# Weights in three pieces, a first state in a bank of its own, and a new order of the first block, in a scan and gated network on one core

## The chip, the cores and the metric

One core of a Trainium2 chip runs the whole program. The metric is device time in microseconds (us). A core has a matrix engine (TensorE, PE in the profile; its weight loads are the row PEld), a vector engine (VectorE, DVE), a scalar engine (ScalarE, ACT), GpSimd (POOL) and SyncE (SP), which here only issues transfers. All work from queues of their own and wait for each other by semaphores. Matrix products land in PSUM, 8 banks of 2 KB per partition; everything else works on SBUF. Sixteen DMA engines move data, fed by queues: q1 (issued by SP), q10 (issued by ScalarE) and q0 (issued by POOL[...]).

## What is computed

The first stage is a linear recurrence with a state, in chunks (Mamba-2), over 4 batches, 8 heads, 768 tokens, head size 32, state size 16. The second is a gated feed-forward network on the 3072 tokens of 256 values, with 1536 hidden units.

```python
for c in range(nc):
    cum = np.cumsum(la, axis=-1)                      # la: log of the decays a
    L = np.exp(cum[..., :, None] - cum[..., None, :]) * causal
    M = np.einsum('bhin,bhjn->bhij', Cc, Bc) * L
    y_intra = np.einsum('bhij,bhjd->bhid', M, xc)
    y_inter = np.einsum('bhin,bhnd->bhid', Cc, state) * np.exp(cum)[..., None]
    y[:, :, sl] = y_intra + y_inter
    Bx = np.einsum('bhjn,bhjd->bhjnd', Bc, xc) * decay_from_j[..., None, None]
    state = decay_full[..., None, None] * state + np.sum(Bx, axis=2)
...
gate = np.maximum(x @ w_gate, 0.0)
out = (gate * (x @ w_val)) @ w_out
```

## The kernel before

**Tiling.** The scan runs in pairs of 128-token chunks, 12 pairs of 256 tokens, three to a batch. The network runs in 6 blocks of 512 tokens, so block 0 needs pairs 0 and 1. The hidden units are 12 tiles f of 128. Decays enter as running products that scale B and C (C by the product, B by its reciprocal), so that the chunk's product of C and B needs only a causal mask.

**A pair of batch 0.** The pairs 0 to 2 take a layout of their own ("wide"). The steps, by name: `load` (C, B and x), `scale_wide` (C or B times the factors `wfac`, the result is the tile bs), `transp` and `tevac` (transposes by TensorE into tp and tpb, copied to BT and CT), `G_wide` (the 4 products g of C and B, a PSUM bank each), `gcopy` and `gmask` (a product is copied by ScalarE and then masked, or masked straight out of PSUM; result gw), `cast_x` (x as bf16), `adds` (the chunk's addition A to the state), `carry` and `pass_on` (the running state T, and its decayed copy Sw for the next chunk), `inter_wide` (C on the old state) and `D_wide` (gw on x), both into the PSUM tiles y and Aps, and `yevac_wide` (the result to yT, the network's input). A of chunk 0 lies in columns 256 to 320 of the y bank. Later pairs use `scale_bc`, `G`, `sums`, `states`, `inter`, `Dm`, `yevac`.

**A block of the network.** `gv` does one tile f for 512 tokens: two products with w_gate, two with w_val, then ScalarE's Relu and VectorE's product (h). `gvh` does the same for one half of the tokens, so that it can start when only one pair is ready; with later=True it returns the VectorE step, to be called later. `fout(b, ts)` multiplies 12 tiles of h by w_out for 128 tokens, and `foevac` copies and stores two of these at a time.

**Order.** It is written out by hand: `in_order` (line 15) keeps every engine's instructions in the order of the program text. So a waiting instruction holds all behind it on its engine. The tile pools add the waits for data and for buffers. Five PSUM banks are shared (`bank`, line 66: dummies, factors, the g products, gv, gate, val, o); one each goes to tp, y and Aps.

**Transfers.** SP issues the loads of inputs; two of them are held by a one-element VectorE memset on their buffer (lines 83 and 96), so they go out only when VectorE has come to that place in its order. POOL issues the weights: `weights(f0, f1)` is one transfer of w_gate and one of w_val, `weights_out` one of w_out. POOL also scales and casts for pair 1 on.

**Dummies.** `keep_warm(n)` runs n products of zeros on TensorE, so that it is not idle while the first pair is prepared.

The main order around the change is at lines 645 to 779; from line 780 a loop does blocks 1 to 5, with the pairs of the next block in between.

Of the kernel before, what the change touches and what calls it, by code (L numbers as in the profile page):

```python
# [29 lines left out]
def kernel(  # L30
# [13 lines left out]
    nc = tc.nc  # L44
# [21 lines left out]
    def bank(name="bank", shape=(128, 512), dtype=FP32):  # L66
        return mm.tile(list(shape), dtype, tag="shared", bufs=NSHARED, name=name)
# [25 lines left out]
    def load_x(p, *qs):  # L93
        xr = raw.tile([128, NH, 2, D], FP32, tag="xr", name="xr")
        if p == 1:
            nc.vector.memset(xr[0:1, 0, 0, 0:1], 0.0)
        n = NH // len(qs)
        for i, q in enumerate(qs):
            hs = slice(i * n, (i + 1) * n)
            q.dma_start(out=xr[:, hs].rearrange("p h r d -> p h (r d)"),  # L100
                        in_=x[0, hs, p * 256:(p + 1) * 256, :].rearrange(
                            "h (p r) d -> p h (r d)", r=2))
        st.setdefault(p, {})["xr"] = xr
# [71 lines left out]
    nc.vector.tensor_copy(  # L175
        heads, oneh.rearrange("p (t q) -> p q t", t=2).to_broadcast([R, 4, 2, N]))

    def keep_warm(n, tag="shared"):
        if tag == "tp":
            w = mm.tile([128, 128], FP32, tag="tp", name="w")  # L180
        else:
            w = bank("w", (128, 128))
        for _ in range(n):
            nc.tensor.matmul(out=w, lhsT=warm, rhs=warm, start=True, stop=True)  # L184

    wg = glob.tile([128, 2, DF], BF16)
    wv = glob.tile([128, 2, DF], BF16)
# [2 lines left out]
    def weights(f0, f1):  # L190
        fs = slice(f0 * 128, f1 * 128)
        for w, src in ((wg, moe_w_gate), (wv, moe_w_val)):
            nc.gpsimd.dma_start(
                out=w[:, :, fs], in_=src[:, fs].rearrange("(k p) f -> p k f", k=2))

    def weights_out(f0, f1):
        nc.gpsimd.dma_start(
            out=wo[:, f0:f1, :],
            in_=moe_w_out[f0 * 128:f1 * 128, :].rearrange("(o i) m -> i o m", i=128))
# [21 lines left out]
    def decays(step):  # L221
        if step == 0:
            nc.vector.tensor_scalar_mul(ends, onew, cp0[:, 127:128])
            return
        d = bank("dec", (128, NC))
        nc.tensor.matmul(out=d, lhsT=heads.rearrange("p q t n -> p (q t n)"), rhs=ends,
                         start=True, stop=True)
        nc.scalar.copy(out=dec, in_=d)
# [8 lines left out]

    def middle():
        nc.vector.reciprocal(rmid, cp[:, H - 1:H])
        nc.vector.tensor_scalar_mul(pick[:, 0], pairs[:, 0], rmid)  # L240

    scaleBC = glob.tile([128, NB, NC, 2, 8], FP32)

# [59 lines left out]
    def cast_x(p, ceng):  # L303
        s = st[p]
        cast = ceng.copy if ceng is nc.scalar else ceng.tensor_copy
        xb = att.tile([128, 2 * NH * D], BF16, tag="xb", name="xb")
        if p < NWIDE:
            cast(xb, s["xr"].rearrange("s h r d -> s (h r d)"))
            s["xb"] = xb.rearrange("s (h r d) -> s h r d", h=NH, r=2)
        else:  # L310
            cast(xb, s["xr"].rearrange("s i h d -> s (i h d)"))
            s["x"] = [xb[:, i * NH * D:(i + 1) * NH * D] for i in range(2)]
# [14 lines left out]
    def tevac(p, beng, ceng):  # L327
# [21 lines left out]
        if p < 2:  # L349
            (beng.copy if beng is nc.scalar else beng.tensor_copy)(BT, tp[0])  # L350

# [16 lines left out]
    def gmask(p, q, eng, psum=False):  # L371
        s = st[p]
        d = s["gw"][:, q]
        m = wmask.unsqueeze(2).to_broadcast([128, 2, 2, 128])
        eng.tensor_tensor(out=d, in0=s["gp"][q] if psum else d, in1=m, op=ALU.mult)  # L375

    def gcopy(p, q):
        s = st[p]
        nc.scalar.copy(out=s["gw"][:, q], in_=s["gp"][q])
# [7 lines left out]
    def adds(p):  # L387
        y_wide(p)
        s = st[p]
        s["A"] = [s["yw"][i][:, 256:320] for i in range(2)]  # L390
        halves = [i for i in range(2) if 2 * p + i < NC - 1]
        for r in range(2):
            for i in halves:
                half = slice(64 * i, 64 * i + 64)
                for q in range(4):
                    nc.tensor.matmul(
                        out=s["A"][i][32 * q:32 * q + 32],
                        lhsT=s["bs"][half, r, 32 * q:32 * q + 32],
                        rhs=s["xb"].rearrange("s (t q) r d -> s q r t d", t=2)[half, q, r],
                        start=r == 0, stop=True,  # L400
                        tile_position=(64 * i, 32 * q), skip_group_check=True)
        for i in halves:
            s["begun"][i] = True

    S = {}
    T_ = {}
# [32 lines left out]
                        tile_position=(32 * q, 32 * q), skip_group_check=True)  # L439
            s["begun"][i] = True  # L440

    def D_wide(p):
        s = st[p]
        for t in range(2):
            for r in range(2):
                for i in range(2):
                    half = slice(64 * i, 64 * i + 64)
                    y = s["yw"][i][:, 0:256].rearrange("s (t m) -> s t m", t=2)
                    for q in range(4):
                        nc.tensor.matmul(  # L450
                            out=y[32 * q:32 * q + 32, t],
                            lhsT=s["xb"][half, 4 * t + q, r], rhs=s["gw"][half, q, r, t],
                            start=not s["begun"][i] and t == 0 and r == 0, stop=True,
                            tile_position=(64 * i, 32 * q), skip_group_check=True)

    def yevac_wide(p, *engs):
        s = st[p]
        for i, eng in enumerate(engs):
            dst = yT[:, :, p * 256 + i * 128:p * 256 + (i + 1) * 128]
            (eng.copy if eng is nc.scalar else eng.tensor_copy)(  # L460
                out=dst, in_=s["yw"][i][:, 0:256].rearrange("s (t m) -> s t m", t=2))
# [161 lines left out]
    def foevac(b, ts):  # L623
        last = b == NBLK - 1
        if ts % 2 == 0 and not last:
            return
        ob = ffn.tile([128, 2, DM], FP32, tag="ob", name="ob", bufs=3)
        r0 = b * 512 + ts * 128
        if last:
            i = ts % 2  # L630
            (nc.vector.tensor_copy if i else nc.scalar.copy)(out=ob[:, i], in_=fst["o"][:, i])
            (nc.sync if i else nc.scalar).dma_start(out=out[r0:r0 + 128, :], in_=ob[:, i])
            return
        nc.scalar.copy(out=ob, in_=fst["o"])  # L634
        nc.sync.dma_start(
            out=out[r0 - 128:r0 + 128, :].rearrange("(i p) m -> p i m", p=128), in_=ob)


    def turn(p, apart=False):
        transp(p, 1, apart)  # L640
        transp(p, 0, apart)

    V, A_, P_ = nc.vector, nc.scalar, nc.gpsimd

    keep_warm(20)
    d = factors()
    decays(0)
    decays(1)
    keep_warm(3)
    nc.vector.tensor_copy(wfac[:, 1], d)  # L650
    nc.gpsimd.tensor_copy(gate[:, 0:1], wfac[0:1, 1, 0, 0, 0:1])
    weights(0, 4)
    scale_wide(0, 1, V)
    nc.vector.reciprocal(wfac[:, 0, :, :, 0], wfac[:, 1, :, :, 0])
    scale_wide(0, 0, V)
    transp(0, 1, False)
    keep_warm(3)
    transp(0, 0, True)
    tevac(0, A_, V)
    nc.vector.reciprocal(wfac[:, 0, :, :, 1], wfac[:, 1, :, :, 1])  # L660
    scan(0, H)
    scale_wide(1, 1, P_)
    weights(4, 8)
    scale_wide(1, 0, P_)
    keep_warm(4)
    G_wide(0)
    keep_warm(16)
    gcopy(0, 0)
    gmask(0, 2, V, True)
    load_x(1, nc.sync)  # L670
    gcopy(0, 1)
    cast_x(0, A_)
    adds(0)
    keep_warm(3)
    gmask(0, 3, V, True)
    gmask(0, 0, V)
    gmask(0, 1, V)
    pass_on(0, 0)
    carry(0, 0)
    middle()  # L680
    inter_wide(0)
    D_wide(0)
    turn(1, True)
    yevac_wide(0, A_, V)
    carry(0, 1)
    weights(8, NF)
    cast_x(1, P_)
    weights_out(0, NF)
    tevac(1, V, A_)
    pass_on(0, 1)  # L690
    def halves(b, u, *fs):
        for f in fs:
            gvh(b, f, u)

    load(2)
    load(3)
    f0 = gvh(0, 0, 0, True)
    G_wide(1)
    decay()
    gcopy(1, 0)  # L700
    gmask(1, 2, V, True)
    f0()
    gcopy(1, 1)
    late = [gvh(0, 1, 0, True)]
    gmask(1, 3, V, True)
    late += [gvh(0, 2, 0, True)]
    adds(1)
    gmask(1, 0, V)
    gmask(1, 1, V)
    carry(1, 0)  # L710
    late += [gvh(0, 3, 0, True), gvh(0, 4, 0, True)]
    pass_on(1, 0)
    late += [gvh(0, 5, 0, True)]
    decay_factors()
    inter_wide(1)
    D_wide(1)
    for fin in late:
        fin()
    nc.vector.reciprocal(wfac[:, 0, :, :, 2], wfac[:, 1, :, :, 2])
    yevac_wide(1, A_, A_)  # L720
    halves(0, 0, 6, 7)
    carry(1, 1)
    pass_on(1, 1)
    load(4)
    load(5)
    scale_wide(2, 1, P_)
# [5 lines left out]
    smask = const.tile([128, 2, 128], BF16)  # L732
    for t in range(2):
        nc.gpsimd.tensor_scalar_mul(smask[:, t], bd, tmask[:, t:t + 1])
    halves(0, 1, 0, 1, 2, 3, 4, 5, 6, 7)
    gv(0, 8)
    gv(0, 9)
    turn(2)
    tevac(2, A_, A_)
    gv(0, 10)  # L740
    gv(0, 11)
    cast_x(2, P_)
    fout(0, 0)
    foevac(0, 0)
# [135 lines left out]
```

## Time and profile before

| What | Value |
|---|---|
| median of 9 runs (range) | 129.48 us (128.66 to 130.27) |
| the profiled execution: time / span | 129.25 us / 127.5 us |
| granted clock of TensorE | 0.997 of full |
| busy share of the span: PE / DVE / ACT / POOL | 95% / 69% / 64% / 31% |
| chain that ended last: PE / DMA / DVE / issue | 80% / 9% / 3% / 2% |
| bytes moved by q1 / q0 | 8.91 / 2.36 MB |
| first products of block 0 (gv) start | 11.19 us |
| first w_out product of block 0 (o) starts | 26.13 us |
| first products of block 1 (gv) start | 34.10 us |

The profile is one execution, in us from the span's start. The page cuts the span into 40 slices of 3.19 us; a digit is the busy share in tenths. A line of the timeline gives start, length, engine (ACTq, SPq and POOLq are issues), line of the program, operation, result and inputs with their shapes, how many instructions are merged (x16), and in brackets how long the engine was idle before and what ended that. A line of the chain gives start, length and what was worked on or waited for. A line of a DMA queue gives packets, MB, and the time of the packets as a share of 16 engines over the stretch asked for.

### The profile page before, as it was taken

Reading aid. Unit: us, or ns where it says so; the run is one execution under the profiler, and the core shown is the slowest. Engines: PE = TensorE matmul, PEld = TensorE weight load, DVE = VectorE, ACT = ScalarE, POOL = GpSimd, SP = SyncE. Lnnn points to the kernel's source line nnn. Section 1 sums busy time; section 2 is a strip of 40 time slices with the busy share of each in tenths; the row PEclk is TensorE's granted clock in tenths of the full one; section 3 lists DMA queues with packets and bytes.
Section 4 is the critical chain, followed back from the end, with each engine's and each line's share of the span. In section 5 each row is a group of like instructions: output and inputs, shape, how many; then the busy total and the mean of one; then the engine's idle time right before and its main releaser. Section 6 shows DMA issues by size and latency. Waiting matters only on the chain.

```text
span 127.5 us, 3631 instructions
## 1 busy us (share of the span) xinstructions
PE 120.9 (95%) x1381; PEld 84.6 (66%) x1387; DVE 88.5 (69%) x201; ACT 81.8 (64%) x186; POOL 40.1 (31%) x84
## 2 busy tenths in 40 slices
PE   6999899899999999999999999999999999999980
PEld 6765577368787468884477874577864677844770
DVE  4896957555799766798674989655989656688420
ACT  0567578654788843887845787935887746877310
POOL 6549402559175008620502802322600033000000
PEclk9999999999999999999999999999999999999998
DMA  3999999998899997197932289912200002200031
GB/s 65 213 152 178 176 212 202 137 126 97 100 114 214 110 124 97 58 162 95 110 50 87 75 108 106 109 27 82 82 5 0 0 0 87 82 0 0 5 115 50
DMA packets 72209, 12.15 MB, mean 95 GB/s; under 512 B 65936, under 2 KB 72192, under 8 KB 72192
## 3 DMA queue, kind: packets, MB, share of 16 engines
q1 hardware_dynamic: 66096, 8.91, 45.5%
q0 software_dynamic: 3184, 2.36, 13.0%
q10 hardware_dynamic: 2912, 0.66, 2.4%
q8 instruction: 11, 0.18, 0.6%
q14 instruction: 6, 0.05, 0.1%
HBM read 11.13 MB, written 3.15 MB: 112 GB/s over the span
## 4 chain that ended last, share of the span: by engine, by line
PE 80%; DMA 9%; DVE 3%; issue 2%; ACT 1%; POOL 1%; SPq 0%; DVEq 0%; POOLq 0%
PE o L618 25%; PE gv L600 16%; PE val L585 14%; PE gate L582 12%; DMA bcr<-in_B_dram 9%; PE w L184 3%; PE y L557 2%; PE tp L325 2%; PE g L469 2%; DVE gs L375 1%; PE y L546 1%; POOL bs L281 1%; PE g L362 1%; PE A_ps L516 1%; DVE h L589 1%
## 5 line engine op out<-in xcount | busy, mean ns | idle before, releaser
L589 DVE TENSOR_TENSOR h<-r,val 128x512 bf16<-128x512 bf16 x42 | 28.0, 684 | 9.6 <-ACT r L588 8.1
L618 PE MATMUL o<-wo,h 128*128 128x256 bf16 x288 | 34.3, 273 | 0.1
L618 PEld LDWEIGHTS <-h 128*128 128x128 bf16 x288 | 27.2, 98 | 5.3 <-issue 1.5
L588 ACT ACTIVATE r<-gate 128x512 bf16<-128x512 f32 x42 | 24.6, 601 | 5.6 <-PE gate L582 3.7
L606 DVE TENSOR_TENSOR h<-r,gv 128x256 bf16<-128x256 bf16 x60 | 23.6, 416 | 4.3 <-ACT r L603 3.7
L585 PE MATMUL val<-yT,wv 128*128 128x512 bf16 x84 | 25.0, 379 | 0.3
L603 ACT ACTIVATE r<-gv 128x256 bf16<-128x256 f32 x60 | 22.6, 384 | 3.3 <-PE gv L600 1.4
L582 PE MATMUL gate<-yT,wg 128*128 128x512 bf16 x78 | 23.7, 379 | 0.0
L600 PE MATMUL gv<-yT,wv 128*128 128x256 bf16 x120 | 22.9, 273 | 0.6 <-DMA wv<-in_moe_w_val_dram 0.6
L600 PE MATMUL gv<-yT,wg 128*128 128x256 bf16 x120 | 23.0, 273 | 0.2
L494 DVE TENSOR_TENSOR gs<-g,maskUT 128x512 bf16<-128x512 f32 x18 | 11.6, 686 | 11.8 <-issue 9.6
L477 POOL TENSOR_SCALAR_AFFINE_SELECT gs<-gs 128x512 bf16<-128x512 bf16 (+1 forms) x18 | 8.9, 520 | 33.0 <-ACT gs L488 33.0
L295 POOL TENSOR_TENSOR bs<-bcr,scaleBC 128x256 bf16<-128x256 f32 x18 | 11.0, 630 | 20.2 <-DMA bcr<-in_C_dram 11.5
L585 PEld LDWEIGHTS <-wv 128*128 128x128 bf16 x84 | 8.2, 98 | 9.9
L600 PEld LDWEIGHTS <-wv 128*128 128x128 bf16 x120 | 11.6, 98 | 2.3 <-DMA wv<-in_moe_w_val_dram 0.8
L600 PEld LDWEIGHTS <-wg 128*128 128x128 bf16 x120 | 11.0, 98 | 2.2 <-issue 0.2
L582 PEld LDWEIGHTS <-wg 128*128 128x128 bf16 x84 | 7.8, 98 | 6.5
L488 ACT CAST gs<-g 128x512 bf16<-128x512 f32 x9 | 5.3, 589 | 6.7 <-PE g L469 6.7
L634 ACT COPY ob<-o 128x512 f32<-128x512 f32 x10 | 5.8, 583 | 5.1 <-PE o L618 5.1
L570 ACT CAST yT<-y 128x512 bf16<-128x512 f32 x9 | 5.3, 585 | 5.2 <-PE y L557 2.5
L184 PE MATMUL w<-warm 128*128 128x128 bf16 x49 | 6.4, 311 | 1.1 <-DVE tmask L155 1.1
L281 POOL TENSOR_TENSOR bs<-bcr,wfac 128x128 bf16<-128x128 f32 x8 | 3.1, 407 | 10.3 <-DVE h L606 6.3
(100 smaller groups left out, 118.7 us busy)
## 6 DMA issues: line engine op xcount, KB each, us to landing
out_dram<-ob SPq DMA_DIRECT2D x10, 256.0 KB, 2.2
xr<-in_x_dram SPq DMA_DIRECT2D x19, 128.0 KB, 3.6
bcr<-in_C_dram SPq DMA_DIRECT2D x19, 64.0 KB, 3.3
bcr<-in_B_dram SPq DMA_DIRECT2D x19, 64.0 KB, 3.5
wg<-in_moe_w_gate_dram POOLq DMA_DIRECT2D x3, 256.0 KB, 5.5
wv<-in_moe_w_val_dram POOLq DMA_DIRECT2D x3, 256.0 KB, 6.0
wo<-in_moe_w_out_dram POOLq DMA_DIRECT2D x1, 768.0 KB, 11.6
xr<-in_x_dram SPq DMA_DIRECT2D x2, 256.0 KB, 8.1
```

What stands on the lines that cost most here:

```text
L184: nc.tensor.matmul(out=w, lhsT=warm, rhs=warm, start=True, stop=True)
L295: eng.tensor_tensor(out=bs.rearrange("s k (q t n) -> s k t q n", q=4, t=2)[:, :, t], in0=src[:, :, t], in1=f[:, :, 4 * t:4 * t + 4].to_bro ...
L477: nc.gpsimd.affine_select(out=dst, in_=dst, pattern=[[0, n], [1, 128]], compare_op=ALU.is_ge, fill=0.0, base=0, channel_multiplier=-1)
L494: nc.vector.tensor_tensor(out=d[:, q], in0=g[q], in1=m, op=ALU.mult)
L582: nc.tensor.matmul(out=g, lhsT=wg[:, k, fs], rhs=yT[:, k, tk], start=(k == 0), stop=(k == 1))
L585: nc.tensor.matmul(out=v, lhsT=wv[:, k, fs], rhs=yT[:, k, tk], start=(k == 0), stop=(k == 1))
L588: nc.scalar.activation(r, g, AF.Relu)
L589: nc.vector.tensor_tensor(out=fst[b][:, f], in0=r, in1=v, op=ALU.mult)
L600: nc.tensor.matmul(out=gv_[:, j], lhsT=w[:, k, fs], rhs=yT[:, k, tk], start=(k == 0), stop=(k == 1), skip_group_check=True)
L603: nc.scalar.activation(r, gv_[:, 0], AF.Relu)
L606: nc.vector.tensor_tensor(out=fst[b][:, f, u * 256:(u + 1) * 256], in0=r, in1=gv_[:, 1], op=ALU.mult)
L618: nc.tensor.matmul(out=o[:, ts % 2], lhsT=fst[b][:, f, ts * 128:(ts + 1) * 128], rhs=wo[:, f], start=(f == 0), stop=(f == NF - 1), skip_gr ...
```

## The change

It has eight parts, all before block 1.

1. The weights come as tiles 0-1, 2-5 and 6-11, not as three pieces of four tiles. The first two pieces are issued one after the other, the third after `load(2)` and `load(3)` in the text. w_out is issued later, behind a mask that POOL does for pair 1.
2. x of pair 1 is loaded earlier in the order, and so are the loads of pairs 2 and 3 (behind `yevac_wide(0)`).
3. Dummies: other numbers, and two groups that read a masked product (gw) instead of zeros, so that they start only when it is there.
4. A of chunk 0 gets a bank of its own, A0. `D_wide` can do some of the q apart.
5. `decays(1)` and the cast of x of pair 0 move to between the two copies of products on ScalarE; `middle` does its second step on POOL.
6. In pair 1 `adds` and the carry come earlier, one mask goes to POOL, and the first-half tiles 1 to 5 stand in another order.
7. Tiles 6 and 7 of block 0 are done for 512 tokens at a time, like 8 to 11.
8. The transposes of pair 2 come one tile f earlier, with its copies spread between the tiles that follow; the copy of the third and fourth o of block 0 is split in two.

```diff
-    def keep_warm(n, tag="shared"):
...
+    def keep_warm(n, rhs=warm):
+        w = bank("w", (128, 128))
         for _ in range(n):
-            nc.tensor.matmul(out=w, lhsT=warm, rhs=warm, start=True, stop=True)
+            nc.tensor.matmul(out=w, lhsT=warm, rhs=rhs, start=True, stop=True)
...
-        nc.vector.tensor_scalar_mul(pick[:, 0], pairs[:, 0], rmid)
+        nc.gpsimd.tensor_scalar_mul(pick[:, 0], pairs[:, 0], rmid)
...
+    def copy_B(p, eng):
+        s = st[p]
+        s["BT"] = BT = att.tile([128, 2, 128], BF16, tag="BT", name="BT")
+        (eng.copy if eng is nc.scalar else eng.tensor_copy)(BT, s["tp"][0])
+
+    def copy_C(p, t):
...
+        nc.scalar.mul(
+            s["CT"].rearrange("s t i m -> s t (i m)")[:, t].rearrange(
+                "s (m r) -> s m r", r=2),
+            s["tp"][1].rearrange("s r m -> s m r"), tmask[:, t:t + 1])
...
+        if p == 0:
+            s["A"][0] = bank("A0", (128, 2 * D))
...
-            s["begun"][i] = True
+            s["begun"][i] = p > 0 or i > 0
...
-    def D_wide(p):
+    def D_wide(p, qs=(0, 1, 2, 3)):
...
-                    for q in range(4):
+                    for q in qs:
...
         if ts % 2 == 0 and not last:
+            if ts and not b:
+                fst["ob"] = ob = ffn.tile([128, 2, DM], FP32, tag="ob", name="ob", bufs=3)
+                nc.scalar.copy(out=ob[:, 0], in_=fst["o"][:, 0])
             return
...
+        if b == 0 and ts == 3:
+            nc.scalar.copy(out=ob[:, 1], in_=fst["o"][:, 1])
+        else:
+            nc.scalar.copy(out=ob, in_=fst["o"])
...
-    keep_warm(20)
+    keep_warm(22)
     d = factors()
     decays(0)
-    decays(1)
-    keep_warm(3)
+    keep_warm(8)
...
-    weights(0, 4)
+    weights(0, 2)
+    weights(2, 6)
...
-    keep_warm(3)
+    keep_warm(4)
...
-    nc.vector.reciprocal(wfac[:, 0, :, :, 1], wfac[:, 1, :, :, 1])
+    nc.vector.reciprocal(wfac[:, 0, :, :, 1:3], wfac[:, 1, :, :, 1:3])
     scan(0, H)
     scale_wide(1, 1, P_)
-    weights(4, 8)
     scale_wide(1, 0, P_)
-    keep_warm(4)
+    load_x(1, nc.sync)
+    keep_warm(6)
     G_wide(0)
-    keep_warm(16)
+    keep_warm(7)
     gcopy(0, 0)
     gmask(0, 2, V, True)
-    load_x(1, nc.sync)
+    keep_warm(5, st[0]["gw"][:, 0, 0, 0])
+    cast_x(0, A_)
+    decays(1)
+    adds(0)
     gcopy(0, 1)
-    cast_x(0, A_)
-    adds(0)
-    keep_warm(3)
     gmask(0, 3, V, True)
+    keep_warm(4, st[0]["gw"][:, 3, 0, 0])
...
-    D_wide(0)
+    D_wide(0, (2, 3, 0))
+    D_wide(0, (1,))
     turn(1, True)
+    keep_warm(2)
     yevac_wide(0, A_, V)
+    load(2)
+    load(3)
     carry(0, 1)
-    weights(8, NF)
+    weights(6, NF)
     cast_x(1, P_)
-    weights_out(0, NF)
...
-    load(2)
-    load(3)
     f0 = gvh(0, 0, 0, True)
     G_wide(1)
     decay()
+    adds(1)
...
-    late = [gvh(0, 1, 0, True)]
     gmask(1, 3, V, True)
-    late += [gvh(0, 2, 0, True)]
-    adds(1)
+    carry(1, 0)
+    pass_on(1, 0)
+    gmask(1, 1, P_)
+    weights_out(0, NF)
     gmask(1, 0, V)
-    gmask(1, 1, V)
-    carry(1, 0)
-    late += [gvh(0, 3, 0, True), gvh(0, 4, 0, True)]
-    pass_on(1, 0)
-    late += [gvh(0, 5, 0, True)]
-    decay_factors()
+    late = [gvh(0, f, 0, True) for f in (1, 2, 3)]
     inter_wide(1)
     D_wide(1)
-    for fin in late:
+    late[0]()
+    late[1]()
+    yevac_wide(1, A_, V)
+    late += [gvh(0, f, 0, True) for f in (4, 5)]
+    for fin in late[2:]:
         fin()
-    nc.vector.reciprocal(wfac[:, 0, :, :, 2], wfac[:, 1, :, :, 2])
-    yevac_wide(1, A_, A_)
-    halves(0, 0, 6, 7)
-    carry(1, 1)
-    pass_on(1, 1)
+    decay_factors()
...
-    halves(0, 1, 0, 1, 2, 3, 4, 5, 6, 7)
+    halves(0, 1, 0, 1, 2, 3, 4, 5)
+    gv(0, 6)
+    carry(1, 1)
+    gv(0, 7)
+    pass_on(1, 1)
     gv(0, 8)
+    turn(2)
+    copy_B(2, A_)
     gv(0, 9)
-    turn(2)
-    tevac(2, A_, A_)
+    copy_C(2, 0)
     gv(0, 10)
     gv(0, 11)
+    copy_C(2, 1)
```

More of the change, by code (lines that the diff above doesn't have):

```diff
@@ L176 @@
         heads, oneh.rearrange("p (t q) -> p q t", t=2).to_broadcast([R, 4, 2, N]))
-    def keep_warm(n, tag="shared"):
[L179 to L182, printed above, removed]
+    def keep_warm(n, rhs=warm):
+        w = bank("w", (128, 128))
         for _ in range(n):
-            nc.tensor.matmul(out=w, lhsT=warm, rhs=warm, start=True, stop=True)
+            nc.tensor.matmul(out=w, lhsT=warm, rhs=rhs, start=True, stop=True)
     wg = glob.tile([128, 2, DF], BF16)
@@ L350, in tevac @@
             (beng.copy if beng is nc.scalar else beng.tensor_copy)(BT, tp[0])
+    def copy_B(p, eng):
[3 more added lines that the diff above has]
+    def copy_C(p, t):
+        s = st[p]
+        if t == 0:
+            s["CT"] = att.tile([128, 2, 2, 128], BF16, tag="CT", name="CT")
+        nc.scalar.mul(
+            s["CT"].rearrange("s t i m -> s t (i m)")[:, t].rearrange(
+                "s (m r) -> s m r", r=2),
+            s["tp"][1].rearrange("s r m -> s m r"), tmask[:, t:t + 1])
     def G_wide(p):
@@ L625, in foevac @@
         if ts % 2 == 0 and not last:
+            if ts and not b:
+                fst["ob"] = ob = ffn.tile([128, 2, DM], FP32, tag="ob", name="ob", bufs=3)
+                nc.scalar.copy(out=ob[:, 0], in_=fst["o"][:, 0])
             return
-        ob = ffn.tile([128, 2, DM], FP32, tag="ob", name="ob", bufs=3)
+        ob = fst.pop("ob", None) or ffn.tile([128, 2, DM], FP32, tag="ob", name="ob", bufs=3)
         r0 = b * 512 + ts * 128
@@ L633, in foevac @@
             return
-        nc.scalar.copy(out=ob, in_=fst["o"])
+        if b == 0 and ts == 3:
+            nc.scalar.copy(out=ob[:, 1], in_=fst["o"][:, 1])
+        else:
+            nc.scalar.copy(out=ob, in_=fst["o"])
         nc.sync.dma_start(
```

## The prediction

> **What bounds the kernel now.** I read the chain of waits first, then TensorE's weight loads and ScalarE in order of time, and last the DMA queues by stretch. The chain from 0 to 42 us:
>
> ```profile
> 10.20 0.79 POOL bs L281 x2
> 11.04 0.30 PE tpb L325 x2
> 11.37 0.29 DVE BT L350
> ...
> 12.13 11.18 DMA bcr<-in_B_dram
> ...
> 23.81 0.42 POOL bs L281
> 24.28 0.30 PE tp L325 x2
> ...
> 32.11 1.32 PE o L618 x12
> 33.46 0.59 ACT ob L634
> 34.10 1.96 PE gv L600 x16
> ```
>
> From 34.10 on the chain is TensorE nearly alone, and the change touches nothing there. So block 1's first gv, at 34.10, decides: each us by which it comes earlier shortens the span by one. Before it, one transfer (B of pair 2, issued 12.13, landed 23.31) releases the transposes. TensorE's stalls after its first gv at 11.16 stand in the weight loads:
>
> ```profile
> 15.49 0.11 PEld L600 LDWEIGHTS <-wv 128*128 128x128 bf16 x2 [0.84 <-DMA wv<-in_moe_w_val_dram]
> ...
> 24.27 0.11 PEld L325 LDWEIGHTS <-bs 128*128 128x128 bf16 x2 [0.71 <-POOL bs L281]
> ...
> 27.57 0.10 PEld L618 LDWEIGHTS <-h 128*128 128x128 bf16 x1 [0.36 <-DVE h L589]
> ```
>
> Up to that first gv TensorE mostly waits for a chain through ScalarE; the last two copies of the mask product stand ahead of the cast of x:
>
> ```profile
> 7.07 1.07 ACT L379 CAST gs<-g 128x512 bf16<-128x512 f32 x2 [0.75 <-PE g L362]
> 8.02 0.63 ACT L308 CAST xb<-xr 128x512 bf16<-128x512 f32 x1
> 9.19 0.31 ACT L424 ACTIVATE Sw<-y,dec 128x64 bf16<-128x64 f32 x1 [0.54 <-PE y L396]
> 9.40 0.20 ACT L413 COPY T<-y 128x64 f32<-128x64 f32 x1
> 10.56 0.37 ACT L460 CAST yT<-y 128x256 bf16<-128x256 f32 x1 [0.95 <-PE Aps L450]
> ```
>
> DMA engines, 12 to 15 us (weights alone, though C and B of pair 2 are issued) and 15 to 17.5 us (both queues):
>
> ```profile
> q0 software_dynamic: 534, 0.52, 112.7%
> ```
>
> ```profile
> q0 software_dynamic: 422, 0.41, 99.1%
> q1 hardware_dynamic: 778, 0.10, 35.3%
> ```
>
> The engines are full until 24.7 us, where W_out lands (issued 13.10, 11.6 us). q0 carries weights, q1 all inputs.
>
> [...]pair 2's C, issued 11.71, moves nothing before 15. So a queue of weights holds loads back for a while, and which comes first matters. [...]the separate bank for A0 buys little.
>
> **Part by part.** a) Prologue. 22 dummies for 20: 2 x 0.105 (2.05/20), and they end just where the scan releases the factors (LDW 3.33): +0.19. Eight dummies stand where decays(1) and three were, under VectorE's scaling: 0. Four and six for three and four, ahead of G: six end 0.1 after BT is there, so G comes at 6.65 for 6.37: +0.28, not a sum with the first but holding it. The copy gcopy(0,0) then ends at 7.9. New order on ScalarE: cast of x (0.63) to 8.43, then the copy of decays(1). That waits for dec's two fp32 matmuls, which stand behind five dummies reading the first copied block (7.94 to 8.45) plus a mode change (0.2) and 0.59: 9.19. Behind this waiting copy stand gcopy(0,1), pass_on, carry. ScalarE: dec 9.22 to 9.39, gcopy(0,1) to 9.87, Sw to 10.16 (before: 9.50). VectorE's mask of q=1 ends 10.5 (before 9.59), and D takes q=2,3,0 first, so it stays hidden. inter 10.22, D 10.55, yT on ScalarE 10.56+0.66=11.22, on VectorE to 11.70. First gv 11.82: **+0.66**. Bounds: 0 (dec's matmuls slip in earlier, dummies shorter) and +1.0[...]. I take +0.66, the worked chain.
>
> b) TensorE's order from first gv (T0=11.82) to block 1. Tiles: 0.435 per half (17.39 to 20.01: six), 0.865 per full one (22.17, 23.03). Six halves less eight and six full less four: same columns, 0. Walk: gv 0; G(1) at 12.43, behind CT, as before; decay 12.81 to 13.6; adds +0.35 (xb: POOL ends weights(6,12) 12.6, cast 13.2); gv 1 to 3 to 15.3; inter waits for pass_on(1,0) (carry 15.0, Sw 15.4), 15.5; D 15.9 to 16.15, its POOL mask (1.15, from 14.2) done 15.35; gv 4, 5 to 17.0. r(1 to 3) are queued on ScalarE ahead of yevac, so it runs 16.45 to 16.82 and VectorE's half to 16.93: just in time. Six second halves to 19.66, full 6, 7, 8 to 22.25, transposes 0.45, full 9, 10, 11 to 25.3: W_out product of block 0 starts at **25.3** (before 25.91/26.13, T0 11.16).
>
> What goes: the 0.84 at wv (tiles 2-5 are issued by 7.75, not 10.18; 1024 packets of tiles 0-5 are 1.9+3.2 us of full engines from 6.3, plus 1.1 for x of pair 1: landed by 13.5, needed 14.65). Small first pieces also end the wv wait of gv 0 (landing 11.38): 0.13, lost in T0. Tiles 6-11 need the total of weights that tiles 8-11 needed before (landed 18.6): I take 19.0, needed 19.7 and 20.1. pick on POOL: about 0.5 (0.49 on VectorE), bounds 0.15 and 0.8, under decay's start at 12.8.
>
> c) Pair 2. C, B, x issued at 11.8, 12.3, 12.9, as late as before (11.71). Gain: all weights ahead of them are through sooner (w 2-5 close behind 0-1, before q0 fell to 58.9% share between 9.5 and 12), so q1 starts at about 14 rather than 15, and W_out, issued at 15.3 for 13.1, starts only behind tiles 6-11 at 18. At 311 packets per us (778/2.5) beside weights, 4 us carry 1240 of the 2048 of C and B; the other 800 at 233 per us (before: about 1118 in 4.8 us beside W_out): 21.4, landed **22.2**, bs 23.0. PE wants it at 22.5: stall 0.6. If q1 starts at 13.4, as x of pair 1 did (1.5 us after issue), 1430 are through, landed 21.4, stall 0. I take 0.2. The DMA for the change at the upper end is in the rivals. W_out: before 7.0 us from last weight packet to landing; 18.0+7.0=25.0, needed 25.3 to 25.5: hidden, bounds 24.3 and 25.8.
>
> d) turn(2) between tiles 8 and 9, its copies between 9, 10 and 11: ScalarE has 0.6 of each 0.865, plus 0.37+0.84+0.35 over six periods: 5.2 of 5.6. The last h no longer comes late: -0.36. ob in halves: the bank of o is free 0.2 earlier, first gv of block 1 waits for it at 33.46 to 34.05: -0.2. Remaining from W_out product to block 1: 34.10-26.13-0.56=7.41. pair 3's loads, POOL's scale (30.04 before) and sums are needed some 1.2 earlier; their loads are in at 28.7: hidden with 0.3 to spare.
>
> Sum: 25.3+0.2 (B) +7.41=32.9, against 34.10: **-1.2**. On the profiled execution 129.25 (span 127.5 and 1.75 around it): 128.05; that execution lies 0.23 below the median of 129.48, so in the median of runs 128.05 to 128.3. Forecast **128.2**.
>
> **Rivals.** (1) The prologue costs nothing (chain a at its lower bound): gain 1.8, 127.4. For: dec's matmuls are small; against: three instructions stand behind its copy. (2) Transfer hidden or late all the same: B lands 22.3 to 23.1, or W_out at 26: stall 0.5 to 1.2, 128.6 to 129.4. For: bytes are the same and the engines are full from 6 to 24.7; against: order is better. (3) Slower: q1 does not start before 15[...]: 825 by 18.0, the other 1223 take 5.2 us, B lands 24.0, transposes at 25.0; now three full tiles stand behind them, not two, so the product starts at 27.8, block 1 at 35.2: +1.1, **130.35**. It decides from a landing of 23.0, where block 1 is back at 34.10. For: before, B landed at 23.31 after the same issue time. Against: W_out was in its way from 17.7.
>
> **Numbers.** Forecast 0.55, (1) 0.10, (2) 0.19, (3) 0.16. Below 0.5% (0.65 us) a measurement of this kernel cannot tell it from no change. Forecast and (1) are faster, of (2) 0.05; same 0.14; (3) is slower, 0.16. Own range of the forecast 127.7 to 128.6; for 8 in 10, 127.3 to 129.7.
>
> **What would show it.** First gv at 11.8; no DMA wait at wv; B of pair 2 landed by 22.2; weight loads of the transposes of pair 2 with less than 0.3 idle; product of block 0 at 25.5 with no wait for h; block 1 at 32.9. Wrong, if B lands after 23, if W_out ends the wait at 25.3, or if first gv comes past 12.5.

## The result, and the profile after

The changed kernel is slower: 131.6 us median of 17 runs (129.71 to 132.59), against 129.48 of 54; the ratio is 1.0114, with a 95% interval of 1.0084 to 1.0145. (The ratio leaves out executions in a slower state, the medians don't.) The profiled execution took 131.27 us, its span is 129.5. Block 1's first gv starts at 36.00, before at 34.10: all of the loss (1.9 of 2.0 us of span) is in front of block 1.

The chain of waits after, from 10 to 44 us (start, length, what was worked on or waited for):

```profile
11.86 3.14 issue
...
15.03 0.61 POOL xb L305
...
15.68 0.21 PE y L409 x4
...
15.94 2.67 PE gv L613 x12
...
28.58 1.32 PE o L631 x12
...
36.00 1.99 PE gv L613 x16
```

Pair 2's B and POOL's scale of it are gone from the chain. In their place stands the cast of pair 1's x, after 3.14 us of nothing, and then 12 products of gv, three half tiles, that take 2.67 us: 0.89 per half tile, twice the 0.435 of before. The timeline says what each waited for:

```profile
15.03 0.60 POOL L305 CAST xb<-xr 128x512 bf16<-128x512 f32 x1 [3.17 <-DMA xr<-in_x_dram]
15.68 0.21 PE L409 MATMUL y<-xb,bs 64*32 64x64 bf16 x4 [3.30 <-POOL xb L305]
15.87 0.61 PE L613 MATMUL gv<-yT,wg 128*128 128x256 bf16 x2
...
19.51 0.39 PE L613 MATMUL gv<-yT,wg 128*128 128x256 bf16 x2
```

In the kernel before, the same products of x came without a wait (POOL's cast of x had waited 0.15 us for the transfer):

```profile
13.91 0.21 PE L396 MATMUL y<-xb,bs 64*32 64x64 bf16 x4
```

Now TensorE waits 3.30 us for x, which POOL itself got only at 15.0. The two products after the wait take 0.61 us, the same two at 19.51 take 0.39. The reason stands in the busy time by stretch (length, PE busy, PEld, DVE, ACT, POOL, then the granted clock, DMA share and GB/s):

```profile
12.48:15.89 3.41, 0.21 (x17) 0.17 (x17) 0.82 (x2) 0.20 (x1) 0.86 (x2) 1.00 1.25 207
15.89:19.30 3.41, 3.41 (x65) 2.18 (x60) 1.87 (x4) 1.50 (x4) 2.68 (x4) 0.50 1.29 214
```

From 12.48 to 15.89 TensorE has 0.21 us of work; from 15.89 to 19.30, for 3.41 us, it works at half clock, which begins 0.2 us after the work came back. In the 0.2 us behind 19.30 the clock reads 1.00 again.

Why x came late is in the DMA issues. The load of pair 1's x, first after (issued 7.32), then before (issued 7.93), with the time from issue to landing last:

```profile
xr<-in_x_dram SPq DMA_DIRECT2D x1, 256.0 KB, 7.6
```

```profile
xr<-in_x_dram SPq DMA_DIRECT2D x1, 256.0 KB, 4.5
```

Issued 0.6 us earlier, it lands 2.5 us later (14.9, not 12.4). The account of block 1's start, from the two traces: +3.3 (x), +1.4 (gv 1 to 3 in 2.67 us, not 1.31), -0.61 (first gv at 10.55, not 11.16), -0.84 (wv of tile 4), -0.71 (transposes of pair 2), -0.36 (h), -0.2 (bank of o): +2.0, measured +1.9. The terms are differences of two single executions, and they hang together: the 0.84 and the 0.71 are gone while TensorE waits for x, and the runs below show that such waits return once it doesn't.

### The profile page after: what moved, and what is told of

Read it like the earlier page. It is cut to its first block, busy times and chain, and to the rows that moved or that the text cites. A ratio compares the mean times of both kernels' runs of the same rounds, so it can differ in the third digit from the quotient of the medians.

```text
span 129.5 us, 3630 instructions
## 1 busy us (share of the span) xinstructions
PE 120.5 (93%) x1382; PEld 84.4 (65%) x1388; DVE 88.4 (68%) x197; ACT 81.8 (63%) x184; POOL 42.1 (33%) x86
## 4 chain that ended last, share of the span: by engine, by line
PE 87%; POOL 6%; issue 3%; DVE 1%; DVEq 0%; POOLq 0%
PE o L631 25%; PE gv L613 20%; PE val L598 15%; PE gate L595 14%; PE y L570 2%; PE g L482 2%; PE w L181 2%; PE tp L322 2%; POOL wg L190 2%; POOL wv L190 2%; POOL bs L278 2%; PE y L559 1%; PE A_ps L529 1%; PE y L463 1%; POOL xb L305 0%
## 5 line engine op out<-in xcount | busy, mean ns | idle before, releaser
L602 DVE TENSOR_TENSOR h<-r,val 128x512 bf16<-128x512 bf16 x44 | 29.5, 685 | 8.8 <-ACT r L601 7.2
L601 ACT ACTIVATE r<-gate 128x512 bf16<-128x512 f32 x44 | 25.9, 600 | 6.0 <-PE gate L595 4.0
L598 PE MATMUL val<-yT,wv 128*128 128x512 bf16 x88 | 26.2, 379 | 0.3
L595 PE MATMUL gate<-yT,wg 128*128 128x512 bf16 x82 | 24.9, 379 | 0.0
L619 DVE TENSOR_TENSOR h<-r,gv 128x256 bf16<-128x256 bf16 x56 | 22.5, 418 | 3.2 <-ACT r L616 2.3
L616 ACT ACTIVATE r<-gv 128x256 bf16<-128x256 f32 x56 | 21.4, 385 | 3.4 <-PE gv L613 1.4
L613 PE MATMUL gv<-yT,wg 128*128 128x256 bf16 x112 | 22.2, 281 | 0.1
L613 PE MATMUL gv<-yT,wv 128*128 128x256 bf16 x112 | 22.1, 281 | 0.0
L181 PE MATMUL w<-warm 128*128 128x128 bf16 x49 | 5.5, 284 | 1.1 <-DVE tmask L155 1.1
L181 PEld LDWEIGHTS <-warm 128*128 128x128 bf16 x58 | 5.0, 126 | 1.8 <-DVE tmask L155 1.0
```

The source lines that it names most:

```text
L181: nc.tensor.matmul(out=w, lhsT=warm, rhs=rhs, start=True, stop=True)
L595: nc.tensor.matmul(out=g, lhsT=wg[:, k, fs], rhs=yT[:, k, tk], start=(k == 0), stop=(k == 1))
L598: nc.tensor.matmul(out=v, lhsT=wv[:, k, fs], rhs=yT[:, k, tk], start=(k == 0), stop=(k == 1))
L601: nc.scalar.activation(r, g, AF.Relu)
L602: nc.vector.tensor_tensor(out=fst[b][:, f], in0=r, in1=v, op=ALU.mult)
L613: nc.tensor.matmul(out=gv_[:, j], lhsT=w[:, k, fs], rhs=yT[:, k, tk], start=(k == 0), stop=(k == 1), skip_group_check=True)
```

## The experiments

My theory: pair 1's x lands late because the weights of tiles 2-5 are now in front of it at the DMA engines, and the new order has nothing on TensorE to do meanwhile, since adds(1) stands ahead of tiles 1 to 3; the idle stretch then costs the clock. Rivals: the new order costs time whatever x does; or the low clock is a matter of its own. Ratios are to the kernel before on the same chip, with 95% intervals; b1 is the start of block 1's first gv in the chain of the profiled execution (34.10 before, 36.00 after). b1 and the waits come from one execution each, and some of these lie off their median (x first 129.44 us against 128.86, w_out at 14.7 129.16 against 128.11, old dummies 127.88 against 129.10), so small differences of b1 don't rank versions.

**x first.** `load_x(1)` ahead of the first weights, the rest as changed.

```diff
+    load_x(1, nc.sync)
     weights(0, 2)
     weights(2, 6)
...
-    load_x(1, nc.sync)
     keep_warm(6)
```

> The changed kernel with the load of x of pair 1 issued ahead of the first weights (at about 4.4 us, not 7.32). My theory (x of pair 1 lands at 14.9 behind tiles 2-5, adds(1) stands in front of everything on TensorE and waits 3.3 us, and the idle stretch halves the granted clock for about 3.8 us more): x lands by about 10, the cast is done at about 12.5, adds(1) waits less than 0.3 us and the clock stays at 1.0. Next late is the second piece of weights (w_val landed 14.8, needed about 13.4): 1.4 to 1.8 us at tile 2. First gv of block 1 at about 32.6, not 36.0; time about 127.9, ratio to before 0.985 to 0.99. Rival (the new order itself costs the time, whatever x does): about as the changed kernel, 131, ratio 1.01.

0.9965 (0.9938 to 0.9992), b1 33.74: 1.5% faster than the changed kernel, the theory's side, by less than it said. x was issued behind pair 1's C at about 4.4 and landed 4.9 us later, adds(1) did not wait for it, the mean clock was 0.996. So the new order doesn't cost the time whatever x does. In the weight loads two other waits came forward:

```profile
14.16 0.11 PEld L613 LDWEIGHTS <-wv 128*128 128x128 bf16 x2 [0.74 <-DMA wv<-in_moe_w_val_dram]
...
23.44 0.11 PEld L322 LDWEIGHTS <-bs 128*128 128x128 bf16 x2 [1.64 <-POOL bs L278]
```

The first was expected, at half its size. The second was not: without the wait for x, POOL reaches w_out's issue at 14.3 rather than 16.7, and pair 2's B lands at 22.5 rather than 19.5.

**adds late.** The transfers as changed, `adds(1)` and what follows behind tiles 1 to 3.

```diff
-    adds(1)
     gcopy(1, 0)
...
     gmask(1, 3, V, True)
+    late = [gvh(0, f, 0, True) for f in (1, 2, 3)]
+    adds(1)
     carry(1, 0)
...
-    late = [gvh(0, f, 0, True) for f in (1, 2, 3)]
```

> The changed kernel with adds(1) (and the carry behind it) put behind the first-half tiles 1 to 3 on TensorE, as the kernel before had it behind tiles 1 and 2; the transfers stay as they are. My theory: x still lands at about 14.9 and is cast at 15.6, but TensorE has three tiles in the meantime; it waits about 1.4 us for w_val of tiles 2-5 (landed 14.8) and then under 0.5 us for x; no idle stretch over 2 us, clock 1.0. Block 1 at about 33.0, time about 128.3, ratio 0.99. Rival (x early or late does not matter, the transfers of weights are what is late): the same 3 us wait at another instruction, about 131.

0.9974 (0.9943 to 1.0006), b1 33.37. x landed at 14.4, late as ever; TensorE lost 0.54 us to wv of tile 2 and 0.3 to x. The gain over the changed kernel is there, though smaller than the 0.99 expected. So a late x costs little where three tiles cover it, and early adds cost no wait where x is there; together they cost 3.3 us of waiting.

**Dummies in the gap.** 32 dummies, then 16, between decay and adds(1); every wait stays.

```diff
     decay()
+    keep_warm(32)
     adds(1)
```

> The changed kernel with 32 dummy products (3.4 us at 0.105) in the gap between decay and adds(1), which leaves every wait as it is and only keeps TensorE busy. It tells the lost clock from the wait: if the half clock from 15.7 to 19.5 comes of the 3.3 us of idleness, the clock stays at 1.0 and the time falls by about 1.7 us less up to 0.3 of overrun: 129.6 to 129.9, ratio 1.00. If the low clock has another cause, 131 and the same dip in the row of the clock.

> The changed kernel with 16 dummy products in the gap between decay and adds(1), not 32: some 1.7 us of dummies and then about 2.5 us of idleness (32 of them left 1.1 us). If the clock falls only after some 3 us of idleness it stays at 1.0 and the time is that of 32 dummies, ratio 1.003; if any long gap costs clock in proportion, the clock dips for one to two us and the ratio is 1.006 to 1.009.

With 32: 1.0034 (1.0006 to 1.0062), b1 34.39, mean clock 1.00. The wait for x is all there (adds at 15.62), so 1.6 us of b1 were the clock's alone. With 16: 1.0175 (1.0105 to 1.0244), b1 36.02: both of my expectations for it were wrong, it gained nothing. The stretches tell why; first 32 dummies, then 16:

```profile
13.21:16.62 3.41, 2.28 (x47) 2.07 (x45) 0.99 (x3) 0.36 (x2) 1.66 (x2) 1.00 1.26 203
```

```profile
12.64:16.05 3.41, 1.14 (x33) 1.00 (x31) 0.74 (x3) 0.10 (x1) 1.01 (x2) 1.00 1.25 208
16.05:19.46 3.41, 3.41 (x60) 2.13 (x58) 1.85 (x4) 1.50 (x4) 2.54 (x4) 0.50 1.27 210
```

The loss isn't in proportion to the wait: after 2.25 us of it (16 dummies) the clock read 0.50 for 3.41 us, as long as after the 3.29 us of the changed kernel; after 1.11 us (32 dummies) it stayed at 1.00. Each run holds one such wait, so these runs don't tell whether its length or the little work around it decides; they show that 2.25 us were enough.

**The split alone.** The kernel before with only the weights' pieces changed.

```diff
-    weights(0, 4)
+    weights(0, 2)
+    weights(2, 6)
...
-    weights(4, 8)
...
-    weights(8, NF)
+    weights(6, NF)
```

> The kernel before with the weights alone changed: tiles 0-1, 2-5 and 6-11 at the places that the changed kernel has them (the first two pieces one behind the other, the third where tiles 8-11 stood). My theory: x of pair 1, issued at 7.9, then lands at about 15 rather than 12.4 and w_val of tiles 2-5 at 14.8; in this order tiles 1 and 2 stand before adds, so tile 2 waits 1.3 us for w_val at 13.3 and adds another 0.8 us for x; the old wait of 0.84 us for w_val of tile 4 is gone. Block 1 about 1.3 us later (a little less if pair 2's B comes earlier): ratio about 1.005 to 1.01. Rival (the split helps by itself and only the moved adds hurts): faster than before, ratio 0.993.

1.0070 (1.0046 to 1.0095), in the range that the theory gave, but b1 is 34.48, 0.38 later and not 1.3: x took 6.0 us to land (13.9), and adds waited 1.16 us. Of the waits expected the one for wv of tile 2 did not come; one of 1.06 for wv of tile 6 did. On the other side the 0.84 at wv of tile 4 and the 0.71 at the transposes were gone. The split makes x late in the old order too, and doesn't help by itself.

**The weights behind x.** The other way round: x at its place, tiles 2-5 issued later.

```diff
     weights(0, 2)
-    weights(2, 6)
...
     scale_wide(1, 1, P_)
+    weights(2, 6)
     scale_wide(1, 0, P_)
```

> The changed kernel with x of pair 1 issued where it was (7.3), and weights of tiles 2-5 behind pair 1's scaled C on POOL (issue at about 8.5 and 9.2, not 6.35 and 7.1). If x is late because these weights stand before it at the DMA engines, x lands at 11 to 12 (before: 4.5 us after its issue), adds(1) does not wait, and w_val of tiles 2-5 lands at about 15, so tile 2 waits some 1.7 us[...]; time 128.5 to 130, ratio 0.993 to 1.005. If x is late for another reason (its own issue time), it still lands at about 15, and the ratio stays at 1.01.

1.0049 (1.0018 to 1.0079), b1 34.89. x, issued at 7.4, landed 3.3 us later (10.7):

```profile
xr<-in_x_dram SPq DMA_DIRECT2D x1, 256.0 KB, 3.3
```

The weights in front of it are what made it late, its issue time is not. (The 0.42 us left at adds(1) are for POOL's cast, which stood behind the issue of tiles 6-11.) But the time went elsewhere: 1.17 us at wv of tile 2, 0.96 at wv of tile 6, 1.17 at w_out.

**w_out held.** Does w_out's issue time decide when pair 2's B lands? A one-element memset on VectorE holds the transfer: in the kernel with x first (to 15.5, shown), and alone in the kernel before (to 16.0, there behind tile 3's step).

```diff
-    weights_out(0, NF)
     gmask(1, 0, V)
...
     late[0]()
     late[1]()
+    nc.vector.memset(wo[0:1, 0, 0:1], 0.0)
+    weights_out(0, NF)
```

> The changed kernel with x of pair 1 ahead of the weights, and the transfer of w_out held by a one-element VectorE memset until tile 2 of the first half is done (issue at about 16, not 14.3). With x early, B of pair 2 landed at 22.5 and the transposes of pair 2 waited 1.6 us; with w_out at 16.2 (adds behind the tiles) it landed at 18.9 and they waited for nothing. Theory (w_out's issue time decides when B lands): B by about 20, the 1.6 us at the transposes gone, w_out lands at about 24.5 and block 1 starts at about 32.3: time about 127.5, ratio 0.985. Rival (B is late because x goes first and takes its place in the queue): B stays at 22 or later, ratio 0.996.

> The kernel before with the transfer of w_out alone held, until tile 3 of the first half is done (issue at about 15.9, not 13.1). Theory: B of pair 2 lands by about 20.5 rather than 23.3, and the transposes of pair 2 don't wait (0.7 us less); w_out lands at about 24.7, needed 25.5: ratio 0.994. If B is late for another reason it stays at 23 and the ratio is 1.0; if w_out is now the late one, over 1.0.

With x first: 0.9886 (0.9834 to 0.9938), b1 32.56, 127.89 us median of 4 runs. This is the lowest ratio of the study, below both kernels; the intervals of the four versions built on it, below, overlap with it. B landed 9.0 us after its issue at 11.1, the transposes did not wait, and the last wait of block 0 is now w_out itself:

```profile
13.94 0.11 PEld L613 LDWEIGHTS <-wv 128*128 128x128 bf16 x2 [0.63 <-DMA wv<-in_moe_w_val_dram]
24.97 1.21 PEld L631 LDWEIGHTS <-h 128*128 128x128 bf16 x12 [1.02 <-DMA wo<-in_moe_w_out_dram]
```

Alone in the kernel before: 0.9944 (0.9886 to 1.0003), b1 33.51; B landed 7.8 us after its issue, not 11.2, and the 0.71 us at the transposes are gone. The interval, from three runs, just touches 1; the trace shows the wait gone.

**Further cuts.** w_out at 14.7 (the two lines above `late[0]()`); four pieces of weights (0-1, 2-3, 4-7 behind both of pair 1's scales, 8-11 behind the cast of its x), both on top of x first and w_out held:

> The version with x of pair 1 first and w_out held, with the hold shorter: w_out goes out at about 14.8, between 14.3 (B of pair 2 landed 22.5, transposes waited 1.6 us) and 15.5 (B landed 20.2, but w_out itself landed at 24.9 and TensorE waited 1.0 us for it). If the order in which the two ask for the DMA engines sets both landings, this lies between: w_out by 24.5, B by 21.0, needed 21.5, waits of 0.5 us at most: ratio 0.984 to 0.987. If B falls back to 22.5 as soon as w_out is earlier, 0.992.

> The same with the weights as tiles 0-1, 2-3, 4-7 and 8-11 (4-7 behind pair 1's B on POOL, the cast of pair 1's x ahead of 8-11). Theory: w_val of tiles 2-3 lands by 13 and the wait of 0.7 us at tile 2 is gone; tiles 4-7 land by about 15.5, needed from 15.2, so up to 0.4 us is left there: block 1 at about 31.9, ratio 0.980 to 0.985. Rival (the weights' total decides, a smaller piece in front only moves the wait to tile 4): same as the run before within 0.3%.

0.9924 (0.9900 to 0.9947), b1 33.32, and 0.9957 (0.9904 to 1.0010), b1 33.77. Both missed what I hoped for, and in the traces w_out's own lateness even grew. In the first w_out landed at 25.7, though issued 0.8 us earlier, and wv of tiles 6-11 was late by 1.14 us. In the second the wait at tile 2 is gone, 0.22 us are left at tile 4, and w_out made TensorE wait 1.82 us, to 26.2. The rival that the total decides fits best: a piece moved forward moves the wait.

**Two parts by themselves.** From the version with x first and w_out held: A of chunk 0 back in the y bank, and the old numbers of dummies (20, 3, 3, 4).

```diff
-        if p == 0:
-            s["A"][0] = bank("A0", (128, 2 * D))
...
-            s["begun"][i] = p > 0 or i > 0
+            s["begun"][i] = True
```

> The same with w_out held to 15.5, and A of chunk 0 back in the y bank (the change's part 4 undone). The forecast had this part at nothing. [...]0 to 0.1 us, ratio 0.9885 as with the own bank. If the own bank matters, D starts 0.3 us later or more.

> The version with x of pair 1 first and w_out held to 15.5, with the numbers of the first four groups of dummies as before the change (20, 3, 3, 4 for 22, 8, 4, 6). With the new numbers the weight loads of the later dummies took 0.056 us each from about 6.8 us on[...], in the kernel before 0.10 us until 8.6[...]. [...]the five and seven later dummies take 0.10 us each here and first gv comes 0.3 to 0.7 us later (11.1 to 11.5, not 10.8); the wait for w_out at the product of block 0 shrinks by the same amount, so the time moves by less than 0.3 us, ratio 0.989 to 0.993. If the new order alone made the prologue shorter, first gv stays at 10.8 and the dummies keep 0.056 us.

Without the own bank: 0.9931 (0.9900 to 0.9962), b1 32.48; D's weight loads start at 9.45 and with the bank at 9.56, in both 0.22 us after those of inter: the bank shows no effect. With the old dummies: 0.9951 (0.9921 to 0.9981), b1 32.57, where the version it starts from had 32.56. First gv came at 11.2 and not 10.8, as expected, and TensorE's pace differed; the seven dummies behind G(0), first with the new numbers ahead of them, then with the old:

```profile
6.88 0.39 PEld L181 LDWEIGHTS <-warm 128*128 128x128 bf16 x7 [0.20 <-issue]
```

```profile
6.95 0.66 PEld L181 LDWEIGHTS <-warm 128*128 128x128 bf16 x7 [0.38 <-issue]
```

Whether either ratio is really worse stays open: the intervals of the three overlap. In the one profiled execution with the old dummies the later start used up the 0.63 us at wv of tile 2, and the wait for w_out ends at 24.98, as it did before (24.97).

## Why the prediction was wrong

The forecast was 128.2 (127.3 to 129.7) and faster; it is 131.6 and slower. The step from block 1's first gv to the time held (1.9 of 2.0 us); what failed lies in front of it.

**The step that failed** is in b), in the brackets behind adds: "xb: POOL ends weights(6,12) 12.6, cast 13.2". I took x of pair 1 as landed when POOL comes to it, because before it took 4.5 us. Under "What goes" I counted its packets among those to be moved with the weights, as "plus 1.1 for x of pair 1", but never asked what stands ahead of x itself: the 1024 packets of tiles 0-5, which I had put at 5.1 us of full engines from 6.3 in the same sentence. That sum, used for x, would have said a landing at 13.5, a cast by 14.1 and a wait of some 0.5 us after decay at 13.6. The wait was 3.30 because decay was over by 12.4 and because the sum was short as well: x and the weights landed only at 14.8 to 14.9. Why that took 1.3 us longer stays open. x was in front of tiles 4-7 before, now it is among tiles 2-5; it landed at 14.9. Runs with x first, with the weights behind x, and with the split alone show it from three sides. Because the change had also put adds ahead of three tiles, nothing covered it. None of my rivals named this transfer: one watched the prologue, two watched pair 2's B and w_out.

**A second cost was left out.** I priced waits at their length. The run with 32 dummies puts 1.6 us of block 1's delay on the half clock after the wait (36.00 against 34.39). The length of the stretch says the same: 3.41 us at 0.50 are 1.7 us less of work, an estimate from the trace of the changed kernel. Why the low clock lasted 3.41 us in both traces that have it, and began at 15.89 and at 16.05, was not shown.

**a)** First gv came at 10.55, not 11.82; the forecast's +0.66 was -0.61 against the one trace of before. The mis-sized term is the price of a dummy, 0.105 us, taken from the first twenty. It fell on the way; in the changed kernel from 0.12 us each to 0.063:

```profile
5.06 0.47 PEld L181 LDWEIGHTS <-warm 128*128 128x128 bf16 x4
5.73 0.38 PEld L181 LDWEIGHTS <-warm 128*128 128x128 bf16 x6
```

The seven behind G(0) took 0.056 us each there and in the version with x first and w_out held; in the four traces with the old numbers, one of which has the new order, those behind G(0) took 0.094 to 0.101. So the faster pace came earlier where more dummies stood ahead; the row of the granted clock reads 1.00 in the prologue of both kernels, so what sets the pace was not shown. The chain through dec's products behind them, worked at 9.19, was over by 8.3. First gv itself spreads, from 10.55 to 11.33 with the new numbers and from 10.82 to 11.20 with the old, so the 0.61 is no measure of the gain; but no trace has the loss that was forecast, and my bounds for it, 0 and +1.0, did not hold the changed kernel's.

**b), the rest.** The wait of 0.84 us for wv is gone, but not because tiles 2-5 landed by 13.5: they landed at 14.8 (7.06 and 7.7 us), and x's wait hid it. With x first it showed as 0.74. Tile order, halves and full tiles cost nothing, as said: from 19.57 to the product of block 0 at 28.58 the chain has no wait above 0.05 us.

**c)** B was to land at 22.2 and landed at 19.5. W_out was to land at 25.0 and did, by luck: it was issued at 16.7, 1.4 us later than forecast, and took 8.3 us, 1.4 less. That a later w_out helps B was right, as the two runs that hold it show; I put it down to a start at 18 behind tiles 6-11 either way, and missed that POOL's waiting moves w_out's issue: at 14.3 B is late, at 15.5 w_out is. Before, q1 moved 778 packets beside 422 of q0 from 15 to 17.5 us, 1.8 to one: that shows that both queues moved, and not how they shared the engines. The stall of 0.2 that I took for B was avoided only by the wait for x; with x first it was 1.64.

**d)** Held in size: from the first product of block 0 to block 1 it took 7.42 us in the chain (28.58 to 36.00), 7.52 in the timeline, forecast 7.41. A0 at nothing was right, as far as the one run without it shows. The 0.2 us that a) of the forecast takes for a change of tiling mode is the size of TensorE's pauses in the kernel before: 0.20 us ahead of D (loads at 9.89) and 0.20 to 0.21 at other changes of the tile's shape, but not at all of them (9.01, from 64x32 to 128x128, has none).

So two costs that the forecast did not have came to 4.7 us, against gains of 2.7 in the trace. Not all of these gains are the change's own: with x first the costs were gone, but waits of 0.74 and 1.64 us came back, and b1 stood at 33.74, not 32.9. The new order's transfers were priced too low in more than one place.

## What to carry to other kernels

A transfer's time to landing is not its own (the same load of x took 3.3 and 7.6 us): when the order of transfers changes, work out for each one, also those that the change hardly moves, what is now in front of it, and who waits. An instruction moved ahead of its neighbours on an in-order engine loses the cover that they gave; move it only after its input's landing has been checked in the new order. Where transfers fill the DMA engines (in the kernel before until 24.7 us), an order is a choice of who waits: look for the one whose wait falls where another engine has work, and price a long TensorE wait above its length (here 1.6 us more, at a wait of 3.29).

## What the runs showed of the hardware

In the traces of two kernels the clock of TensorE read 0.50 for one stretch of 3.41 us, beginning 0.2 to 0.35 us after work began again, behind waits of 3.29 and 2.25 us; behind one of 1.11 us it stayed at 1.00. At this place nothing between 1.11 and 2.25 was tried. In half of the changed kernel's 18 executions the mean clock is 0.971 to 0.974, in the others 0.981 to 0.987; one such stretch at half clock is 1.3% of the span, so the former may have lost two. That is an estimate: no trace of them was kept.

A load of 256 KB, issued at 7.3 to 7.4, took 7.6 us to land, and 3.3 when the weights of tiles 2-5 were moved behind it. Pair 2's B took 11.2 us in the kernel before and 7.8 in the same kernel with w_out held, issued near 12.1 in both.
